# Exponentiating the first batch's keys before the transpose instead of after the maximum

## The chip, the cores and the metric

The kernel runs on one core of one Trainium2 chip. The metric is the device time of one execution in microseconds (us). The kernel before took a median of 944.75 us over three runs (944.59, 944.75 and 946.4).

Five engines of the core matter here. TensorE (PE in the profile, PEld for its weight loads) multiplies and transposes, VectorE (DVE) and ScalarE (ACT) do the elementwise work, GpSimd (POOL) fills constants and issues some DMAs, and SyncE (SP) issues most of the DMAs.

## The reference

A linear attention feeds a gated layer. All arrays are float32.

```python
batch, n_heads, seq, head_dim = (8, 8, 576, 64)
n_tokens, d_model, d_ff = (4608, 512, 1536)

q_s = np.exp(q - np.max(q, axis=-1, keepdims=True))
q_s = q_s / (np.sum(q_s, axis=-1, keepdims=True) + 1e-09)
k_s = np.exp(k - np.max(k, axis=2, keepdims=True))
k_s = k_s / (np.sum(k_s, axis=2, keepdims=True) + 1e-09)
kv = np.einsum('bhsd,bhse->bhde', k_s, v)
x = np.einsum('bhsd,bhde->bhse', q_s, kv)
# heads are joined to 512 features per token; x is (4608, 512)
gate = 1.0 / (1.0 + np.exp(-(x @ w_gate)))
out = (gate * (x @ w_val)) @ w_out
```

The queries are normalised over the 64 features of a head, the keys over the 576 positions of a batch. `max` and `sum` of the keys therefore run along the sequence.

## The kernel before, in words

The 4608 tokens are cut into nine windows of 512 (`w`, `T`). Each window needs its attention output `x` (512 features by 512 tokens, four tiles of 128 features), and then the layer: twelve blocks `j` of 128 hidden units, each with a gate and a value product (`g1_0`, `g1`) and a product back (`g2_0`, `g2`) into four PSUM accumulators.

Windows 1 to 8 run a scheme with fewer block products and split operands; they make up the span from about 162 us on. Window 0 runs plainly (`g1_0(j)`, `g2_0(j)`, lines 644 to 682) because at its time the weights are still being loaded and narrowed. The weights arrive as 64-bit words; `w_low`, `w_top` and `w_join` (and `wo_low`, `wo_top`, `wo_join`) turn them into float32, partly on VectorE, partly on ScalarE. While TensorE works on window 0, those two engines narrow, sum and split the weights of all twelve blocks.

Order is written out by hand: each engine executes its instructions in the order of the code, and SP issues its DMAs in the order of the code. At most eight of SP's DMAs are in flight: the ninth waits until the first has landed, and so on. The loads at the start are, in order: batch 0's keys `k0` (positions on partitions, two tiles per DMA), its queries `q0`, the first weights `w_raw(0)`, batch 0's values `v0`, then `wo(0)`, `w(1)`, `wo(1)`, `w(2)`, batch 1's transposed keys, `w(3)`, `wo(2)`, window 1's queries; after the start stage `w(4)`, batch 1's keys, and from block to block one `wo` and one `w`.

The start stage is what lies ahead of `g1_0(0)`, lines 909 to 1029. With positions on partitions the keys' maximum has to run across partitions. So VectorE takes the maximum over the five position tiles (L960, L963), TensorE transposes the result (L966), VectorE reduces it (L971) and spreads it on a diagonal (L974), TensorE multiplies the diagonal by ones to have the maxima on all partitions (L980), and VectorE subtracts them from each tile (L379) before ScalarE exponentiates it (L384). The queries are treated between these steps: `qn_max` (L473), `qn_sub` (L480), `qn_exp` (L484), `qn_sum` (L490 to L496), `qf_mul` (L521), and `qf_tr` (L527) transposes them. `k_mm_0` (L392) multiplies keys by values, two groups `g` of two feature tiles; the values carry one column of ones more per head pair (129 columns), whose result is the keys' sum. `k_done_0` (L423 to L415) divides by that sum. `x_mm_0` (L589) multiplies by the queries, and `x_ev_0` takes the result out of PSUM as `x_0`, on which `g1_0(0)` works.

`warm(n)` (L955) issues n products of ones that nobody reads. A float32 product stands in the profile as two matmuls, a transpose as one.

Of the kernel before, what the change touches and what calls it, by code (L numbers as in the profile page):

```python
# [52 lines left out]
def attn_moe(ctx: ExitStack, tc: tile.TileContext, qf, qn, qT, k, kT, v, wg, wv, wo, out):  # L53
# [297 lines left out]
    def k_load(b, t, kt=None):  # L351
        s0, n = KTILES[t]
        if kt is None:
            kt = ring.tile([P, DM], F32, name="ring")
        nc.sync.dma_start(out=kt[:n], in_=k[b, s0:s0 + n])
        kt_sb[b, t] = kt

    def v_load(b, t, vt=None):
# [8 lines left out]
        src = v[b, s0:s0 + n]
        if b == 0:
            nc.sync.dma_start(out=vt[:n, :, 0:P], in_=src.rearrange("s (h e) -> s h e", e=P))
        else:  # L370
            nc.sync.dma_start(out=vt[:n], in_=src)

    def k_sub(b, t, eng=nc.vector):
        n = KTILES[t][1]
        kt, m = kt_sb[b, t][:n], kmb[b][:n]
        if b > 0:
            kt = kt.rearrange("s (h p) -> s h p", p=P)
            m = m.rearrange("s (p h) -> s h p", h=NP)
        eng.tensor_tensor(out=kt, in0=kt, in1=m, op=ALU.subtract)  # L379

    def k_exp(b, t):
# [2 lines left out]
        nc.scalar.activation(kt[:n], kt[:n], AF.Exp)  # L384

    def k_mm_0(t, g, ps):

        n = KTILES[t][1]
        kt, vt = kt_sb[0, t], v_sb[0, t]
        for i in range(2):  # L390
            hp = 2 * g + i
            nc.tensor.matmul(  # L392
                ps[:, i], lhsT=kt[:n, hp * P:(hp + 1) * P], rhs=vt[:n, hp],
                start=(t == 0 and i == 0), stop=(t == len(KTILES) - 1 and i == 1),
                skip_group_check=True,
            )
# [73 lines left out]
    def qn_max(w, c):  # L470
        if c == 0:
            q_m[w] = const.tile([P, NC * TI, 1], F32, name="q_m")
        nc.vector.tensor_reduce(  # L473
            out=q_m[w][:, c * TI:(c + 1) * TI], in_=qn_sb[w, c], axis=AX.X, op=ALU.max
        )

    def qn_sub(w, c, eng=nc.vector):
        t = qn_sb[w, c]
        m = q_m[w][:, c * TI:(c + 1) * TI]
        eng.tensor_tensor(out=t, in0=t, in1=m.broadcast_to([P, TI, D]), op=ALU.subtract)  # L480

    def qn_exp(w, c):
        t = qn_sb[w, c]
        nc.scalar.activation(t, t, AF.Exp)  # L484
# [436 lines left out]
    for t in (ones, v0[:, :, :, P:VW]):  # L921
        nc.gpsimd.memset(t, 1.0)

    for t in range(0, 4, 2):
        rows = k[0, t * P:(t + 2) * P].rearrange("(t p) e -> p t e", p=P)
        nc.sync.dma_start(out=k0[:, t:t + 2], in_=rows)
        kt_sb[0, t], kt_sb[0, t + 1] = k0[:, t], k0[:, t + 1]
    k_load(0, 4, k0[:, 4])
    for c in range(0, NC, 2):
        nc.sync.dma_start(out=q0[:, c:c + 2], in_=qf[0, c:c + 2].rearrange("c p t -> p c t"))  # L930
    for c in range(NC):
        qn_sb[0, c] = q0[:, c].rearrange("p (i d) -> p i d", d=D)
# [20 lines left out]
    def warm(n):  # L953
        for _ in range(n):
            nc.tensor.matmul(idle[:, 0:P], lhsT=ones, rhs=ones, start=True, stop=True)  # L955
# [4 lines left out]
    nc.vector.tensor_tensor(out=top, in0=k0[:, 0], in1=k0[:, 1], op=ALU.max)  # L960
    for t in range(2, 5):
        n = KTILES[t][1]
        nc.vector.tensor_tensor(out=top[:n], in0=top[:n], in1=kt_sb[0, t][:n], op=ALU.max)  # L963
    ps = ps_acc.tile([P, DM], F32, name="acc")
    for hp in range(NP):
        nc.tensor.transpose(ps[:, hp * P:(hp + 1) * P], top[:, hp * P:(hp + 1) * P], ident)  # L966
    warm(6)
    qn_max(0, 0)
    qn_max(0, 1)
    m = const.tile([P, NP, 1], F32, name="kmax_0")  # L970
    nc.vector.tensor_reduce(  # L971
        out=m, in_=ps.rearrange("p (h s) -> p h s", s=P), axis=AX.X, op=ALU.max
    )
    nc.vector.tensor_tensor(  # L974
        out=diag.rearrange("p (h s) -> p h s", s=P),
        in0=ident.unsqueeze(1).broadcast_to([P, NP, P]),
        in1=m.broadcast_to([P, NP, P]), op=ALU.mult,
    )
    kmb[0] = ps_acc.tile([P, DM], F32, name="acc")
    nc.tensor.matmul(kmb[0], lhsT=ones, rhs=diag, start=True, stop=True)  # L980
    qn_max(0, 2)
    qn_max(0, 3)
    for c in range(NC):
        qn_sub(0, c)
    for c in range(2):
# [1 line left out]
    k_sub(0, 0, nc.vector)
    nc.scalar.copy(out=wide, in_=kmb[0])
    k_exp(0, 0)
    kmb[0] = wide  # L990
# [200 lines left out]
```

## Time and profile before

| what | value |
|---|---|
| median of three runs | 944.75 us |
| the profiled execution's own time | 946.96 us |
| its span, first to last instruction | 945.2 us |
| around the span (946.96 less 945.2) | 1.76 us |
| mean granted TensorE clock | 0.994 |
| PE busy over the span | 933.5 us, 99% |
| first matmul of `g1_0(0)` starts at | 31.77 us |

The profile is one execution. A row of a group gives line, engine, operation, output and inputs by the program's names, shapes, the count (x), then the time busy in us, the mean in ns of one, and the engine's idle time ahead of them with what ended it. A row of the timeline or of the chain of waits gives the start in us from the start of the span, the length in us, and what ran. A row of a table by stage gives the stretch, busy time per engine with counts in brackets, the granted TensorE clock (1.00 is full), the DMA engines' busy share, and GB/s moved. L12 is line 12 of the kernel. A DMA row gives the KB of one and the us from issue to landing.

### The profile page before, as it was taken

The page shows a single profiled execution, that of the slowest core. Times are in us where ns is not written, and L with a number is a line of the kernel's source. Part 1 is how long each engine was busy: PE and PEld are TensorE (multiplying, and loading weights), DVE is VectorE, ACT ScalarE, POOL GpSimd, SP SyncE. Part 2 cuts the span into 40 slices and gives each one's busy share as a digit, 9 for nine tenths or more (in the row PEclk, how much of TensorE's full clock was granted, in tenths as well). Part 3 has the DMA queues.
Part 4 walks back from the last instruction along what each step waited for, and adds up shares of the span by engine and source line. Part 5 has one row for each costly group of instructions (what it writes and reads, how often), then busy time and mean ns, then how long its engine had stood idle before and what let it go on. Part 6 is the DMA issues. An engine that isn't in the chain of part 4 may idle for free.

```text
span 945.2 us, 15707 instructions
## 1 busy us (share of the span) xinstructions
PE 933.5 (99%) x6062; PEld 808.2 (86%) x6062; DVE 626.4 (66%) x1017; ACT 485.4 (51%) x822; POOL 176.5 (19%) x330
## 2 busy tenths in 40 slices
PE   6999999999999999999999999999999999999998
PEld 5545545899999999999999999999999999999997
DVE  8899879874767477755776568556856664654242
ACT  4799786635455445544563456254725443543222
POOL 0011112222121212212221122112212122222220
PEclk8999999999999999999999999999999999999999
DMA  9996576999699969996999699978997789858661
GB/s 323 328 392 226 210 288 237 362 342 272 185 372 320 264 183 354 335 266 208 333 331 283 204 309 344 287 246 252 351 266 229 221 258 314 238 177 262 212 212 67
DMA packets 94249, 256.74 MB, mean 272 GB/s; under 512 B 13600, under 2 KB 15904, under 8 KB 94176
## 3 DMA queue, kind: packets, MB, share of 16 engines
q0 software_dynamic: 46016, 167.27, 56.6%
q1 hardware_dynamic: 48160, 88.48, 30.9%
q8 instruction: 48, 0.79, 0.4%
q14 instruction: 25, 0.20, 0.1%
HBM read 227.15 MB, written 28.56 MB: 271 GB/s over the span
## 4 chain that ended last, share of the span: by engine, by line
PE 98%; DVE 1%; DMA 1%; ACT 0%; issue 0%; SPq 0%; DVEq 0%
PE gv L695 49%; PE acc L763 28%; PE gv L650 9%; PE acc L677 4%; PE at L405 3%; PE gv L565 2%; PE at L565 1%; PE acc L392 1%; DMA lent<-k_in 1%; PE acc L589 0%; PE gv L527 0%; DVE lent L480 0%; DVE q_m L473 0%; DVE lent L963 0%; ACT lent L384 0%; ACT lent L484 0%
## 5 line engine op out<-in xcount | busy, mean ns | idle before, releaser
L695 PE MATMUL gv<-c_hl,s_sb 128*128 128x256 f32 x2304 | 277.6, 276 | 0.0
L695 PEld LDWEIGHTS gv<-c_hl,s_sb 128*128 128x128 f32 x2304 | 269.1, 188 | 0.0
L695 PE MATMUL gv<-c_hl,a_w 128*128 128x256 f32 x1728 | 221.0, 277 | 0.0
L695 PEld LDWEIGHTS gv<-c_hl,a_w 128*128 128x128 f32 x1728 | 210.5, 188 | 4.6 <-issue 0.7
L301 POOL DMA_DIRECT2D s_sb<-s x188 | 101.3, 539 | 306.2 <-PE gv L695 299.8
L721 DVE TENSOR_TENSOR sg<-gv,sg 128x512 f32<-128x512 f32 x48 | 33.2, 691 | 167.5 <-PE gv L695 167.5
L763 PE MATMUL acc<-wo_hl,h 128*128 128x512 f32 x588 | 142.4, 391 | 0.0
L763 PE MATMUL acc<-wo_t,h 128*128 128x512 f32 x564 | 138.9, 394 | 0.0
L763 PEld LDWEIGHTS acc<-wo_t,h 128*128 128x128 f32 x564 | 105.8, 188 | 24.8
L763 PEld LDWEIGHTS acc<-wo_hl,h 128*128 128x128 f32 x588 | 106.9, 188 | 20.7
L713 ACT COPY sg<-gv 128x512 f32<-128x512 f32 x48 | 28.1, 585 | 118.1 <-PE gv L695 104.7
L723 ACT COPY sg<-gv 128x512 f32<-128x512 f32 x48 | 28.2, 587 | 102.8 <-PE gv L695 102.8
L725 DVE TENSOR_TENSOR sg<-sg 128x512 f32<-128x512 f32 x48 | 33.2, 692 | 57.1 <-ACT sg L723 57.1
L650 PE MATMUL gv<-x,f_w 128*128 128x512 f32 x160 | 70.3, 593 | 0.0
L248 POOL DMA_DIRECT2D wo_hl<-wo x47 | 27.6, 588 | 194.8 <-PE acc L763 194.8
L650 PEld LDWEIGHTS gv<-x,f_w 128*128 128x128 f32 x160 | 30.0, 190 | 36.6 <-issue 34.4
L746 DVE TENSOR_TENSOR h<-sg,h 128x1024 fp32r<-128x1024 f32 x48 | 58.8, 1226 | 1.6
L734 DVE TENSOR_TENSOR sg<-sg 128x512 f32<-128x512 f32 x48 | 33.2, 692 | 33.5 <-ACT sg L728 33.5
L728 ACT ACTIVATE sg<-sg 128x512 f32<-128x512 f32 x48 | 30.3, 632 | 46.1 <-DVE sg L727 46.1
L718 ACT COPY sg<-gv 128x512 f32<-128x512 f32 x48 | 28.2, 587 | 37.3 <-PE gv L695 37.3
L715 ACT COPY sg<-gv 128x512 f32<-128x512 f32 x48 | 28.2, 587 | 36.5 <-PE gv L695 36.5
L248 POOL DMA_DIRECT2D wo_t<-wo x47 | 25.3, 538 | 99.2 <-PE acc L763 99.1
(153 smaller groups left out, 1151.3 us busy)
## 6 DMA issues: line engine op xcount, KB each, us to landing
s_sb<-s POOLq DMA_DIRECT2D x188, 512.0 KB, 6.2
wo_hl<-wo POOLq DMA_DIRECT2D x47, 512.0 KB, 5.0
wo_t<-wo POOLq DMA_DIRECT2D x47, 512.0 KB, 6.6
s<-s_sb POOLq DMA_DIRECT2D x24, 512.0 KB, 6.7
out<-x SPq DMA_DIRECT2D x36, 256.0 KB, 7.0
ring<-k_in SPq DMA_DIRECT2D x28, 256.0 KB, 9.5
ring<-qn_in SPq DMA_DIRECT2D x28, 256.0 KB, 6.0
q_b<-q_m_row SPq DMA_DIRECT2D x56, 128.0 KB, 9.4
```

What stands on the lines that cost most here:

```text
L248: nc.gpsimd.dma_start(out=t.rearrange("p h e -> p (h e)"), in_=wo_dram[2 * p + i].bitcast(F32R))
L301: nc.gpsimd.dma_start(out=s_sb[:, i].rearrange("p h n e -> p (h n e)"), in_=s_dram[p][:, i * n:(i + 1) * n].bitcast(F32R),)
L405: nc.tensor.matmul(kvps[b][:, hp], lhsT=kt[:n, sl], rhs=vt[:n, sl], start=(t == 0 and hp == 0), stop=(t == len(KTILES) - 1 and hp == NP - ...
L650: nc.tensor.matmul(ps[n], lhsT=w[:, kt // 2, sl], rhs=x_0[:, kt], start=(kt == 0), stop=(kt == NK - 1),)
L677: nc.tensor.matmul(acc[0][m], lhsT=h_0[j][:, m * P:(m + 1) * P], rhs=wo_t[j // 2][:, j % 2], start=(j == 0), stop=(j == NJ - 1),)
L695: nc.tensor.matmul(ps[:, n], lhsT=lh(kt), rhs=c_hl[i][:, x, kt], start=(first and n == 0 and kt == 0 and lh is wh and x == 0), stop=(last ...
L721: nc.vector.tensor_tensor(out=sg[:, 0], in0=rr, in1=sg[:, 0], op=ALU.add)
L725: nc.vector.tensor_tensor(out=sg[:, 3], in0=sg[:, 3], in1=sg[:, 2], op=ALU.add)
L728: nc.scalar.activation(sg[:, 0:2, 0], sg[:, 0:2, 0], AF.Sigmoid)
L734: tt(out=sg[:, 0:2, 0], in0=sg[:, 0:2, 0], in1=sg[:, 0:2, 1], op=ALU.mult)
L746: nc.vector.tensor_tensor(out=lo, in0=sg[:, :, 0], in1=hi.bitcast(F32), op=ALU.subtract)
L763: nc.tensor.matmul(acc[w][m], lhsT=h[lh][:, i, sl], rhs=o[i][:, rh], start=(at == 0 and i == 0 and lh == 0 and rh == 0), stop=(at == NS - ...
```

## The change

Batch 0's keys are now read with features on partitions, `kT`, one DMA for each of the four feature tiles of 128 features by 576 positions, and the loads alternate: two key tiles, two query tiles, two key tiles, two query tiles. The maximum now runs along the free axis: `k_max` (a reduction and a negation on VectorE) and `k_sum` (one exponential on ScalarE, with the maximum as bias and the sum as a second result). The exponentiated tile is then transposed by TensorE, four full pieces of 128 positions and one of 64 (`k_tr_0`), and ScalarE copies it from PSUM (`k_get_0`). The sum comes with the exponential, so the values lose their column of ones: 128 columns instead of 129, and their DMA writes rows of 2048 bytes per partition instead of four of 512.

The filling matmuls are dealt out anew: 11 at the start and 8 after each pair, instead of 16 and 6. `k_mm_0` runs through the position tiles inside a feature tile, no longer through feature tiles inside a position tile. VectorE clears a quarter of `f_last` instead of the whole.

```diff
-    nc.vector.memset(f_last, 0.0)
+    nc.vector.memset(kv_0, 0.0)
     nc.vector.tensor_copy(
-        out=kv_sb.rearrange("p b i h e -> p (b i h e)"),
-        in_=f_last.rearrange("p b n e -> p (b n e)"),
+        out=kv_sb.rearrange("p b i h e -> p (b i) (h e)"),
+        in_=kv_0.rearrange("p h e -> p (h e)").unsqueeze(1).broadcast_to([P, 4, DM]),
     )
...
-        if b == 0:
-            nc.sync.dma_start(out=vt[:n, :, 0:P], in_=src.rearrange("s (h e) -> s h e", e=P))
-        else:
-            nc.sync.dma_start(out=vt[:n], in_=src)
+        nc.sync.dma_start(out=vt[:n], in_=src)
...
+    def k_tr_0(hp):
+        if hp % 2 == 0:
+            k_ps["end", hp // 2] = ps_gv.tile([P, T], F32, name="gv")
+        k_ps[hp] = ps = ps_acc.tile([P, DM], F32, name="acc")
+        for t, (s0, n) in enumerate(KTILES):
+            if n == P:
+                o = ps[:, t * P:(t + 1) * P]
+            else:
+                o = k_ps["end", hp // 2][:n, hp % 2 * P:(hp % 2 + 1) * P]
+            nc.tensor.transpose(o, kT_sb_0[hp][:, s0:s0 + n], ident)
+
+    def k_get_0(hp):
+        nc.scalar.copy(out=k0[:, hp], in_=k_ps.pop(hp))
+        if hp % 2:
+            n = KTILES[-1][1]
+            nc.scalar.copy(
+                out=k0_end[:n, hp - 1:hp + 1].rearrange("s h d -> s (h d)"),
+                in_=k_ps.pop(("end", hp // 2))[:n, 0:2 * P],
+            )
+
+    def k_mm_0(g, ps):
         for i in range(2):
             hp = 2 * g + i
-            nc.tensor.matmul(
-                ps[:, i], lhsT=kt[:n, hp * P:(hp + 1) * P], rhs=vt[:n, hp],
-                start=(t == 0 and i == 0), stop=(t == len(KTILES) - 1 and i == 1),
+            for t, (s0, n) in enumerate(KTILES):
+                kt = k0[:, hp, t * P:(t + 1) * P] if n == P else k0_end[:n, hp]
+                nc.tensor.matmul(
+                    ps[:, i], lhsT=kt, rhs=v_sb[0, t][:n, hp * P:(hp + 1) * P],
+                    start=(t == 0 and i == 0), stop=(t == len(KTILES) - 1 and i == 1),
...
-        k_r = const.tile([P, NP], F32, name="k_r0")
-        nc.vector.tensor_scalar_add(k_r[:, gs].unsqueeze(2), ps[:, :, P:VW], EPS)
-        nc.vector.reciprocal(k_r[:, gs], k_r[:, gs])
+        k_r = ksum[0]
+        if g == 0:
+            nc.vector.tensor_scalar_add(k_r, k_r, EPS)
+            nc.vector.reciprocal(k_r, k_r)
...
+    kT_sb_0 = [k0T[:, hp] for hp in range(NP)]
+    for i in range(0, NP, 2):
+        for hp in (i, i + 1):
+            nc.sync.dma_start(out=k0T[:, hp], in_=kT[0, hp * P:(hp + 1) * P])
+            kT_load(0, hp, k0T[:, hp])
+        for c in (i, i + 1):
+            nc.sync.dma_start(out=q0[:, c], in_=qf[0, c])
+            qn_sb[0, c] = q0[:, c].rearrange("p (i d) -> p i d", d=D)
...
-    warm(16)
+    warm(11)
+
+    for i in range(0, NP, 2):
+        for hp in (i, i + 1):
+            k_max(0, hp)
+            k_sum(0, hp)
+            k_tr_0(hp)
+        for c in (i, i + 1):
+            qn_max(0, c)
+            qn_sub(0, c)
+            qn_exp(0, c)
+            k_get_0(c)
+        warm(8)
     w_low(0)
-    for c in range(2, NC):
-        qn_exp(0, c)
-    for t in range(1, 5):
-        k_exp(0, t)
     w_top(0)
-    kv0 = [ps_acc.tile([P, 2, VW], F32, name="acc") for _ in range(2)]
+    kv0 = [pool.tile([P, 2, P], F32, name=name) for pool, name in ((ps_at, "at"), (ps_acc, "acc"))]
     for g in range(2):
-        for t in range(5):
-            k_mm_0(t, g, kv0[g])
+        k_mm_0(g, kv0[g])
...
-        qf_tr(0, hp, ps_gv.tile([P, T], F32, name="gv") if hp < 3 else
-              ps_at.tile([P, T], F32, name="at"))
+        qf_tr(0, hp, ps_gv.tile([P, T], F32, name="gv"))
```

Left out of the diff are the removed lines of the old maximum (lines 960 to 997 of the kernel before, printed above) and of the old loads of keys and queries, and the places in the lent tiles.

What the order of instructions becomes on TensorE, from the last filling matmuls ahead of the keys-by-values product to `x_mm_0`. Before (L955 is `warm`, L980 the spreading of the maxima, L392 `k_mm_0`, L527 `qf_tr`, L589 `x_mm_0`):

```order
L955 MATMUL gv<-lent 128x128 x6
L980 MATMUL acc<-lent 128x512
L392 MATMUL acc<-lent 128x129 x20
L527 MATMUL gv<-ident,lent 128x128 x12
L527 MATMUL at<-ident,lent 128x128 x4
L589 MATMUL acc<-q_151,f_last 128x512 x2
```

Now (L393 is the transpose of the keys, L971 `warm`, L409 `k_mm_0`, L545 `qf_tr`, L607 `x_mm_0`):

```order
L393 MATMUL acc<-ident,lent 128x128 x4
L393 MATMUL gv<-ident,lent 64x128
L971 MATMUL gv<-lent 128x128 x8
L409 MATMUL at<-lent 128x128 x10
L409 MATMUL acc<-lent 128x128 x10
L545 MATMUL gv<-ident,lent 128x128 x16
L607 MATMUL acc<-q_151,f_last 128x512 x2
```

The single product that spread the maxima, and the wait for it, are gone from TensorE; eight filling matmuls now stand directly ahead of the keys-by-values product, whose columns are 128.

On VectorE, from the subtraction of the queries' maxima to the first scaling of the queries. Before (L480 `qn_sub`, L379 `k_sub`, L146 `w_low(0)`, L490 to L496 `qn_sum`, L521 `qf_mul`):

```order
L480 TENSOR_TENSOR lent<-lent,q_m 128x512 x4
L379 TENSOR_TENSOR lent<-lent,acc 128x512
L379 TENSOR_TENSOR lent<-lent 128x512 x3
L379 TENSOR_TENSOR lent<-lent 64x512
L146 TENSOR_SCALAR w_raw<-w_raw 128x1024
L490 TENSOR_REDUCE q_r<-lent 128x8 x4
L495 TENSOR_SCALAR q_r<-q_r 128x32
L496 RECIPROCAL q_r<-q_r 128x32
L521 TENSOR_TENSOR lent<-lent,q_r 128x512 x2
```

Now (L498 `qn_sub` of the last query tile, L145 `w_low(0)`, L508 to L514 `qn_sum`, L539 `qf_mul`):

```order
L498 TENSOR_TENSOR lent<-lent,q_m 128x512
L145 TENSOR_SCALAR w_raw<-w_raw 128x1024
L508 TENSOR_REDUCE q_r<-lent 128x8 x4
L513 TENSOR_SCALAR q_r<-q_r 128x32
L514 RECIPROCAL q_r<-q_r 128x32
L539 TENSOR_TENSOR lent<-lent,q_r 128x512 x2
```

The five subtractions of the keys' maxima are gone; the narrowing of the first weights follows directly on the queries.

More of the change, by code (lines that the diff above doesn't have):

```diff
@@ L33 @@
 KTILES = [(i * P, min(P, S - i * P)) for i in range((S + P - 1) // P)]
-VW = P + 1
 NF = 2
@@ L375, in k_sub @@
         kt, m = kt_sb[b, t][:n], kmb[b][:n]
-        if b > 0:
-            kt = kt.rearrange("s (h p) -> s h p", p=P)
-            m = m.rearrange("s (p h) -> s h p", h=NP)
+        kt = kt.rearrange("s (h p) -> s h p", p=P)
+        m = m.rearrange("s (p h) -> s h p", h=NP)
         eng.tensor_tensor(out=kt, in0=kt, in1=m, op=ALU.subtract)
@@ L384, in k_exp @@
         nc.scalar.activation(kt[:n], kt[:n], AF.Exp)
-    def k_mm_0(t, g, ps):
-        n = KTILES[t][1]
-        kt, vt = kt_sb[0, t], v_sb[0, t]
+    k_ps = {}
+    def k_tr_0(hp):
[17 more added lines that the diff above has]
+    def k_mm_0(g, ps):
         for i in range(2):
             hp = 2 * g + i
-            nc.tensor.matmul(
-                ps[:, i], lhsT=kt[:n, hp * P:(hp + 1) * P], rhs=vt[:n, hp],
-                start=(t == 0 and i == 0), stop=(t == len(KTILES) - 1 and i == 1),
-                skip_group_check=True,
-            )
+            for t, (s0, n) in enumerate(KTILES):
[3 more added lines that the diff above has]
+                    start=(t == 0 and i == 0), stop=(t == len(KTILES) - 1 and i == 1),
+                    skip_group_check=True,
+                )
     def k_mm(b, t):
@@ L910, in attn_moe @@
     k1T = lent[5][:, 0:NP * S].rearrange("p (h s) -> p h s", s=S)
-    k0 = lent[4][:, 0:5 * DM].rearrange("p (t e) -> p t e", e=DM)
-    ones = lent[4][:, 5 * DM:5 * DM + P]
+    k0T = lent[4][:, 0:NP * S].rearrange("p (h s) -> p h s", s=S)
+    ones = lent[4][:, NP * S:NP * S + P]
+    k0 = lent[0][:, 0:NP * 4 * P].rearrange("p (h s) -> p h s", s=4 * P)
+    k0_end = lent[0][:, NP * 4 * P:NP * 5 * P].rearrange("p (h d) -> p h d", d=P)
     q0 = lent[3][:, 0:NC * T].rearrange("p (c t) -> p c t", t=T)
-    top, diag = (lent[3][:, NC * T + i * DM:NC * T + (i + 1) * DM] for i in range(2))
-    v0 = lent[2][:, 0:5 * NP * VW].rearrange("p (t h e) -> p t h e", t=5, e=VW)
-    wide = lent[0][:, 0:DM]
+    v0 = lent[2][:, 0:5 * DM].rearrange("p (t e) -> p t e", e=DM)
     v1 = [
@@ L920, in attn_moe @@
     ]
[L921 to L932, printed above, removed]
+    nc.gpsimd.memset(ones, 1.0)
+    kT_sb_0 = [k0T[:, hp] for hp in range(NP)]
[6 more added lines that the diff above has]
+            qn_sb[0, c] = q0[:, c].rearrange("p (i d) -> p i d", d=D)
     load_w(0)
@@ L955, in warm @@
             nc.tensor.matmul(idle[:, 0:P], lhsT=ones, rhs=ones, start=True, stop=True)
-    warm(16)
[L960 to L985, printed above, removed]
-        qn_exp(0, c)
[L987 to L990, printed above, removed]
-    for t in range(1, 5):
-        k_sub(0, t)
+    warm(11)
[10 more added lines that the diff above has]
+        warm(8)
     w_low(0)
-    for c in range(2, NC):
-        qn_exp(0, c)
-    for t in range(1, 5):
-        k_exp(0, t)
     w_top(0)
-    kv0 = [ps_acc.tile([P, 2, VW], F32, name="acc") for _ in range(2)]
+    kv0 = [pool.tile([P, 2, P], F32, name=name) for pool, name in ((ps_at, "at"), (ps_acc, "acc"))]
     for g in range(2):
-        for t in range(5):
-            k_mm_0(t, g, kv0[g])
+        k_mm_0(g, kv0[g])
     for c in range(NC):
```

## The prediction

> **What bounds the kernel now.** I read the page first, then the chain of waits over the first 100 us, then a table by stage of the same time.
>
> ```profile
> PE 933.5 (99%) x6062; PEld 808.2 (86%) x6062; DVE 626.4 (66%) x1017; ACT 485.4 (51%) x822; POOL 176.5 (19%) x330
> PE   6999999999999999999999999999999999999998
> ```
>
> TensorE is busy everywhere but in the first of 40 slices. So a change of the start stage is worth what it moves the moment from which TensorE never waits again. The chain says when that is:
>
> ```profile
> 12.38 2.40 DVE lent L480 x4
> ...
> 18.14 8.46 PE acc L392 x36
> 26.60 1.46 PE gv L527 x12
> 28.06 0.44 PE at L527 x4
> 28.50 3.44 PE acc L589 x8
> 31.93 13.73 PE gv L650 x32
> ```
>
> Up to 18 us VectorE's maxima and subtractions end last, with ScalarE's exponentials; then `k_mm_0` holds TensorE. Everything from 31.93 on is TensorE alone. Two things beside it show in the stages (the third last column is the granted clock, the last is GB/s):
>
> ```profile
> 4.00:8.00 4.00, 2.96 (x21) 2.77 (x19) 2.42 (x5) 0.00 (x0) 0.00 (x0) 1.00 1.06 348
> 12.00:16.00 4.00, 0.37 (x1) 0.00 (x0) 3.38 (x6) 1.82 (x4) 0.00 (x0) 0.95 1.24 285
> 20.00:24.00 4.00, 4.00 (x18) 3.55 (x17) 3.83 (x10) 3.03 (x3) 0.00 (x0) 0.50 1.02 406
> 24.00:28.00 4.00, 4.00 (x27) 3.67 (x26) 2.51 (x8) 0.78 (x2) 0.00 (x0) 0.77 1.05 397
> 33.00:36.00 3.00, 3.00 (x8) 1.33 (x7) 2.96 (x7) 3.00 (x4) 0.00 (x0) 1.00 0.64 171
> 32.00:100.00 68.00, 68.00 (x191) 32.74 (x190) 66.60 (x117) 64.14 (x84) 8.15 (x15) 1.00 0.85 309
> ```
>
> First, TensorE sat idle ahead of `k_mm_0` and ran it at a granted clock of 0.50. Second, VectorE is busy 66.60 of the 68 us from 32 to 100: it narrows weights with hardly a gap. Whatever makes VectorE wait there is not made up before 100 us.
>
> **The change, part by part.** The prices of the new work are those of like operations in this trace:
>
> ```profile
> L330 DVE TENSOR_REDUCE k_max<-lent 128x1 f32<-128x576 f32 x4 | 3.0, 740 | 0.0
> L331 DVE TENSOR_SCALAR k_neg<-k_max 128x1 f32<-128x1 f32 x6 | 0.9, 154 | 0.2
> L473 DVE TENSOR_REDUCE q_m<-lent 128x8 f32<-128x512 f32 x4 | 2.5, 672 | 0.0
> L480 DVE TENSOR_TENSOR lent<-lent,q_m 128x512 f32<-128x512 f32 x4 | 2.5, 682 | 0.0
> L146 DVE TENSOR_SCALAR w_raw<-w_raw 128x1024 uint32<-128x1024 uint32 x2 | 1.4, 682 | 0.0
> L490 DVE TENSOR_REDUCE q_r<-lent 128x8 f32<-128x512 f32 x4 | 2.4, 668 | 0.0
> L521 DVE TENSOR_TENSOR lent<-lent,q_r 128x512 f32<-128x512 f32 x4 | 2.6, 689 | 0.1
> L415 DVE TENSOR_TENSOR f_last<-acc,k_r 64x128 f32<-64x128 f32 x4 | 1.2, 289 | 0.1
> L337 ACT ACTIVATE lent<-lent,k_neg 128x576 f32<-128x576 f32 x4 | 3.0, 761 | 0.0
> L484 ACT ACTIVATE lent<-lent 128x512 f32<-128x512 f32 x4 | 2.4, 624 | 3.5 <-DVE lent L480 3.5
> L484 ACT ACT_TABLE_LOAD x1 | 1.3, 1283 | 8.2 <-DMA lent<-qf_in 8.2
> L596 ACT COPY x<-acc 128x512 f32<-128x512 f32 x2 | 1.2, 586 | 1.7 <-PE acc L589 1.7
> ```
>
> *The first keys.* The first load of 512 KB, issued at 0.74, took 3.8 us. A key tile is 288 KB, 0.23 MB less; at the 0.4 MB per us of the stage rows it lands 0.6 earlier, at about 4.0.
>
> ```profile
> 0.74 0.43 SPq L926 DMA_DIRECT2D lent<-k_in  x1
> lent<-k_in SPq DMA_DIRECT2D x1, 512.0 KB, 3.8
> 9.47 2.52 SPq L369 DMA_DIRECT2D lent<-v_in  x1
> lent<-v_in SPq DMA_DIRECT2D x1, 128.0 KB, 7.2
> 90.30 4.66 PE at L405 x40
> ```
>
> *VectorE.* From 4.0 it works without a gap, as the other tiles land 0.7 apart: maxima 3.0, negations 4 x 0.15 = 0.6, queries 2.5 + 2.5, narrowing half of 1.4 = 0.7, sums 2.4, scaling 2.6, four small steps at about 0.2 (like the negations' 0.15) 0.8, the results 1.2. Together 16.3, so it ends at 20.3 and has scaled the last query tile at 19.7, half of the results earlier.
>
> *ScalarE.* From 4.0: the table 1.3, exponentials 3.0 + 2.4, copies at most 6 x 0.59: 10.2, so 14.2, with waits for VectorE about 14.8. It hides behind the values, below; were they there, it would be the next to end.
>
> *The values.* The last landed at 9.47 + 7.2 = 16.7. While they moved, the rows show 285 GB/s, after it 406; 1.18 MB take 4.1 us at the one and 2.9 at the other. In rows of 2048 bytes, as the rest is, they land 1.2 earlier, at 15.5. In the Trainium skill, "DMA: Bandwidth & Descriptors", section Specifications, 512 bytes already suffice for line rate; the 285 against 406 speaks against it here, and by the page the values would still land at 16.7 (a rival, below).
>
> *TensorE.* `k_mm_0` is 40 matmuls; at the full clock L405 gives 4.66/40 = 0.117 each, against 8.46/36 = 0.235 in the chain above. Four of the first five products can run ahead; 32 matmuls after 15.5 end at 19.2. The sixteen transposes take 1.46/12 = 0.12 each, 1.9 in all: `x_mm_0` starts at 21.1 (VectorE's last query tile would allow 20.2). Against 28.50 this is **7.4 us earlier**. The 20 transposes of keys, 2.4 us, fall before 13 us, where TensorE otherwise fills. Bounds: values landing another 0.6 earlier because the 348 of 4 to 8 us also rises to 406, then 20.5 decides, 8.0; values no earlier, 22.3, 6.2.
>
> *What costs nothing.* The fill and cast of `kv_sb` end before the first keys land, as they did (the cast with a repeated source could take twice its time and still would). `x_ev_0`, `w_join` and the rest move along with `x_mm_0`.
>
> *What does not move along: the loads.* SP's queue holds the same bytes in the same order behind the values. The narrowing meets `wo(3)` first:
>
> ```profile
> 37.61 0.33 SPq L138 DMA_DIRECT2D wo_raw<-wo_in  x1
> wo_raw<-wo_in SPq DMA_DIRECT2D x1, 512.0 KB, 6.5
> 44.85 0.42 DVE L146 TENSOR_SCALAR wo_raw<-wo_raw 128x512 uint32<-128x512 uint32 x1
> 84.58 0.68 DVE L662 TENSOR_TENSOR h<-gv,h 128x512 f32<-128x512 f32 x1
> 86.70 0.59 PE L677 MATMUL acc<-wo_t,h 128*128 128x512 f32 x1
> ```
>
> It landed at 44.1, 0.75 before VectorE read it. What it gains: 1.2 from the values, and the thin stretch from 33 to 36 (171 of 400 GB/s, 1.7 us), since `w(4)` waits for VectorE and is issued earlier. That gives 41.2. The other end: 14.2 MB lie up to it (keys and queries 2.2, values 1.2, five w 5.2, four wo 2.1, batch 1's keys twice 2.4, window 1's queries 1.1), at 0.4 MB per us from 2.5 us on 37.9. Nothing tells where between; I take the middle, **39.6**. VectorE then reads it 44.85 - 39.6 = 5.25 earlier, not 7.4, and stays that late. TensorE feels it where VectorE's lead is least: the product at 84.58 ends at 85.26 and its reader starts at 86.70, a lead of 1.44. So TensorE keeps 5.25 + 1.44 = **6.7 us** of the 7.4.
>
> *The sum.* 946.96 - 6.7 = **940.3**. The profiled execution is 2.2 above the median of 944.75 and 0.6 above the longest of the three. The half-clock stretch would account for it: without it `k_mm_0` would not be last, VectorE's last scaling and four transposes would, and `x_mm_0` would start at 25.64 + 0.5, 2.4 earlier.
>
> ```profile
> 24.35 1.29 DVE L521 TENSOR_TENSOR lent<-lent,q_r 128x512 f32<-128x512 f32 x2
> ```
>
> The new kernel is reckoned without that stretch, so its time stands; from the median it is 4.5 away.
>
> **Rivals.**
>
> *No backlog.* The queue runs near its best, or VectorE's lead absorbs the rest: the whole 8.0 arrives, 939.0; if the profiled execution's surplus over the median is the profiler's, 944.75 - 8.0 = 936.8. For it: 0.75 of lead today, and 406 GB/s where rows are long. Against: the lead is smaller than the 7.4 that VectorE moves.
>
> *The values' rows were not it.* 285 GB/s had another cause, and the values land at 16.7: `wo(3)` at 42.4, VectorE gains 2.45, TensorE 3.9: 943.1. The DMA share of 1.24 in that row, the highest, speaks for short rows.
>
> *Slower: the half clock stays.* At the start the clock is not full either:
>
> ```profile
> 1.14 5.82 PE L955 MATMUL gv<-lent 128*128 128x128 f32 x32 [1.14 <-POOL lent L922]
> 16.63 0.77 PE L392 MATMUL acc<-lent 128*128 128x129 f32 x2 [4.26 <-ACT lent L384]
> ```
>
> 32 matmuls took 0.18 each, between the 0.117 and the 0.235: they became fast on the way. Now there are 22, and behind them come short bursts. If these do not bring the full clock, `k_mm_0` takes 40 x 0.235 = 9.4 from 15.8 on, and the rest 1.9 + 3.44: 30.5, a gain of 1.4, 945.5. If the half clock also holds through `qf_tr` and `x_mm_0` (3.8 + 6.9), `g1_0(0)` starts at 35.9, 4.0 later than before: **951.0**. It decides whether the granted clock is 0.50 still at 27 us. Against it: the gaps between bursts are under 2 us, where a gap of 4.26 took the clock away. For it: before, the clock came back only after 7.6 us of steady matmuls (18.14 to about 25.8, by the 0.77). The Trainium skill, "TensorE: Matmul & The Clock Gate", Part 1, gives about 3.4 us of busy time for that, which this trace more than doubles; by the page the first 22 matmuls, 5.2 us at 0.235, bring the full clock and the forecast stands. Part 4 says that transposes do not count as busy, which no run here shows and which would leave these bursts thinner.
>
> **How the numbers follow.** Forecast, full clock with a backlog: 0.60, 939.6 (all 7.4) to 941.9 (`wo(3)` at 41.2). No backlog 0.17. Short rows innocent 0.05. Half clock through `k_mm_0` 0.09, further 0.05. Something unseen 0.04, mostly still a gain. The range takes in the forecast and the low rival's 936.8 and reaches up to the short rows' 943.1: 936.8 to 943.1. About 0.2% (1.9 us) is what a measurement of this kernel can tell from no change. Faster 0.60 + 0.17 + 0.03 = 0.80; within it 0.05 + 0.09 = 0.14; slower 0.06.
>
> **What would show it.** `k_mm_0` at 0.117 per matmul with the granted clock at 1.00 from 12 us on; `x_mm_0` at 21.1; VectorE's idle time ahead of `wo(3)`'s narrowing ended by a DMA, and a short TensorE wait at the fifth product back. I am wrong if `x_mm_0` starts after 23, if VectorE does not wait for a load between 29 and 40 us, or if the clock reads 0.50 after 15 us.

## The result, and the profile after

The changed kernel is slower: 956.2 us as the median of its first measurement against 944.79 for the kernel before, a ratio of 1.0115 with a 95% interval of 1.0095 to 1.0135. One of the four executions, the profiled one, took 4422.31 us with every matmul several times as long; it is left out, and the profile read here is that of the same kernel run again (e1_again: 955.72, ratio 1.0093 [1.0072, 1.0114]). Its span is 953.7 us, 8.5 more than before.

The stages of the start first (stretch; busy time of PE, PEld, DVE, ACT and POOL; granted clock; DMA share; GB/s):

```profile
4.00:8.00 4.00, 3.81 (x27) 3.45 (x26) 3.50 (x7) 3.81 (x7) 0.00 (x0) 1.00 1.03 335
12.00:16.00 4.00, 3.25 (x28) 2.87 (x25) 3.97 (x7) 3.79 (x6) 0.00 (x0) 1.00 1.06 359
20.00:24.00 4.00, 4.00 (x30) 3.40 (x29) 1.55 (x4) 1.56 (x3) 0.00 (x0) 1.00 1.03 399
24.00:28.00 4.00, 4.00 (x11) 1.74 (x10) 3.24 (x6) 2.40 (x3) 0.00 (x0) 1.00 1.04 406
33.00:36.00 3.00, 3.00 (x9) 1.33 (x8) 2.90 (x8) 2.99 (x4) 0.00 (x0) 1.00 1.03 404
32.00:100.00 68.00, 67.43 (x190) 32.28 (x189) 65.74 (x115) 62.08 (x83) 8.68 (x16) 1.00 0.84 308
```

The start stage moved as forecast in kind: the clock reads 1.00 in every one of these stages, the thin stretch from 33 to 36 us now moves 404 GB/s instead of 171, and from 12 to 16 us TensorE is busy for 3.25 us instead of 0.37. (The thin stretch is not the change's alone: a run of the kernel before with the same start instructions, e7 below, whose clock came back earlier, moves 405 there. An earlier start is enough to fill it.) The timeline of TensorE gives the moments (start, length):

```profile
23.41 3.60 PE L607 MATMUL acc<-q,f_last 128*128 128x512 f32 x8
26.84 1.02 PE L668 MATMUL gv<-x,f_w 128*128 128x512 f32 x2
...
157.98 1.95 PE L713 MATMUL gv<-c_hl,a_w 128*128 128x256 f32 x12
159.78 3.00 PE L713 MATMUL gv<-c_hl,s_sb 128*128 128x256 f32 x24
```

The same matmuls of the kernel before:

```profile
28.33 3.60 PE L589 MATMUL acc<-q,f_last 128*128 128x512 f32 x8
31.77 0.59 PE L650 MATMUL gv<-x,f_w 128*128 128x512 f32 x1
162.08 1.15 PE L695 MATMUL gv<-c_hl,a_w 128*128 128x256 f32 x5
```

`x_mm_0` starts 4.9 us earlier, and when windows 1 to 8 begin, at the first product with `c_hl`, 4.1 us of it are still there. Yet the end is 8.5 us later. So 12.6 us were lost behind 158 us, in code that the diff doesn't touch. The groups by line say where. Before:

```profile
L695 PE MATMUL gv<-c_hl,s_sb 128*128 128x256 f32 x2304 | 277.6, 276 | 0.0
L695 PE MATMUL gv<-c_hl,a_w 128*128 128x256 f32 x1728 | 221.0, 277 | 0.0
L763 PE MATMUL acc<-wo_hl,h 128*128 128x512 f32 x588 | 142.4, 391 | 0.0
L763 PE MATMUL acc<-wo_t,h 128*128 128x512 f32 x564 | 138.9, 394 | 0.0
```

And after:

```profile
L713 PE MATMUL gv<-c_hl,s_sb 128*128 128x256 f32 x2304 | 288.1, 281 | 0.0
L713 PE MATMUL gv<-c_hl,a_w 128*128 128x256 f32 x1728 | 222.5, 278 | 0.0
L781 PE MATMUL acc<-wo_hl,h 128*128 128x512 f32 x588 | 142.5, 391 | 0.0
L781 PE MATMUL acc<-wo_t,h 128*128 128x512 f32 x564 | 138.9, 394 | 0.0
```

Same shapes, same counts, no idle time ahead of them, no lower clock (a mean of 1.000 after, 0.994 before): 10.5 us more in the products of `s_sb` (the weights) with `c_hl` (the moving data), 1.5 more in those of `a_w` with `c_hl`, nothing in the products back. Together 12.0 of the 12.6. In the chain of waits the 84 matmuls of a step stand as one piece, before

```profile
211.26 9.52 PE gv L695 x84
...
226.31 9.52 PE gv L695 x84
```

and after

```profile
207.41 9.80 PE gv L713 x84
...
222.73 9.80 PE gv L713 x84
```

which is 113.3 against 116.7 ns per matmul, averaged over a step (9.52/84 and 9.80/84). A step has 48 products of `s_sb` and 36 of `a_w`. By the starts of the matmuls in the trace, one to the next, the former went from 113.7 to 118.3 ns and the latter from 113.9 to 114.7, on average over the whole run. What the change does to these matmuls stands in two lines of the diff that carry no work: the tiles `kmax_0` (L970) and `k_r0` (L422) of the kernel before, 32 bytes per partition each, are gone. Pools are laid out one behind the other, so everything allocated behind these two lies 64 bytes lower in each partition, `c_hl` and `a_w` among it; `s_sb`, the first tile, stays. (All places here are added up from the tiles of the kernel's code; the profile shows none. `c_hl` is several tiles; by its start the first of them is meant, and the others lie multiples of 128 bytes behind it.)

### The profile page after: what moved, and what is told of

Its sections match the earlier page's. It is cut to its first block, busy times and chain, and to the rows that moved or that the text cites. A ratio compares the mean times of both kernels' runs of the same rounds, so it can differ in the third digit from the quotient of the medians.

```text
span 4420.5 us, 15759 instructions
## 1 busy us (share of the span) xinstructions
PE 4415.4 (100%) x6086; PEld 3418.9 (77%) x6086; DVE 626.5 (14%) x1012; ACT 494.3 (11%) x830; POOL 174.1 (4%) x329
## 4 chain that ended last, share of the span: by engine, by line
PE 100%; ACT 0%; issue 0%; POOL 0%; POOLq 0%
PE gv L713 47%; PE acc L781 27%; PE gv L668 11%; PE acc L695 6%; PE at L422 4%; PE gv L583 2%; PE at L583 1%; PE gv L971 1%; PE acc L607 0%; PE gv L545 0%; PE acc L409 0%; PE at L409 0%; PE acc L393 0%; PE gv L393 0%; ACT x L687 0%
## 5 line engine op out<-in xcount | busy, mean ns | idle before, releaser
L713 PE MATMUL gv<-c_hl,s_sb 128*128 128x256 f32 x2304 | 1222.4, 830 | 0.0
L713 PEld LDWEIGHTS gv<-c_hl,s_sb 128*128 128x128 f32 x2304 | 1213.7, 742 | 0.0
L713 PEld LDWEIGHTS gv<-c_hl,a_w 128*128 128x128 f32 x1728 | 931.4, 731 | 39.5 <-issue 37.4
L713 PE MATMUL gv<-c_hl,a_w 128*128 128x256 f32 x1728 | 946.1, 840 | 0.0
L781 PE MATMUL acc<-wo_hl,h 128*128 128x512 f32 x588 | 617.8, 1337 | 0.0
L781 PE MATMUL acc<-wo_t,h 128*128 128x512 f32 x564 | 586.8, 1327 | 0.0
L781 PEld LDWEIGHTS acc<-wo_t,h 128*128 128x128 f32 x564 | 348.3, 618 | 224.0 <-issue 224.0
L781 PEld LDWEIGHTS acc<-wo_hl,h 128*128 128x128 f32 x588 | 362.8, 634 | 196.2 <-issue 191.9
L668 PE MATMUL gv<-x,f_w 128*128 128x512 f32 x160 | 426.3, 3011 | 0.0
L668 PEld LDWEIGHTS gv<-x,f_w 128*128 128x128 f32 x160 | 143.8, 905 | 264.8 <-issue 263.0
L739 DVE TENSOR_TENSOR sg<-gv,sg 128x512 f32<-128x512 f32 x48 | 33.2, 691 | 1901.9 <-PE gv L713 1901.9
L695 PE MATMUL acc<-wo_t,h 128*128 128x512 f32 x96 | 258.4, 3043 | 0.0
L695 PEld LDWEIGHTS acc<-wo_t,h 128*128 128x128 f32 x96 | 89.1, 933 | 161.1 <-issue 161.1
L422 PE MATMUL at<-f_last,ring 128*128 128x128 f32 (+1 forms) x160 | 92.4, 875 | 0.0
L422 PEld LDWEIGHTS at<-f_last,ring 128*128 128x128 f32 (+1 forms) x160 | 88.3, 780 | 4.3 <-issue 4.3
L743 DVE TENSOR_TENSOR sg<-sg 128x512 f32<-128x512 f32 x48 | 33.2, 692 | 291.2 <-ACT sg L741 291.2
```

The costliest lines, as they stand in the source:

```text
L422: nc.tensor.matmul(kvps[b][:, hp], lhsT=kt[:n, sl], rhs=vt[:n, sl], start=(t == 0 and hp == 0), stop=(t == len(KTILES) - 1 and hp == NP - ...
L668: nc.tensor.matmul(ps[n], lhsT=w[:, kt // 2, sl], rhs=x_0[:, kt], start=(kt == 0), stop=(kt == NK - 1),)
L695: nc.tensor.matmul(acc[0][m], lhsT=h_0[j][:, m * P:(m + 1) * P], rhs=wo_t[j // 2][:, j % 2], start=(j == 0), stop=(j == NJ - 1),)
L713: nc.tensor.matmul(ps[:, n], lhsT=lh(kt), rhs=c_hl[i][:, x, kt], start=(first and n == 0 and kt == 0 and lh is wh and x == 0), stop=(last ...
L739: nc.vector.tensor_tensor(out=sg[:, 0], in0=rr, in1=sg[:, 0], op=ALU.add)
L743: nc.vector.tensor_tensor(out=sg[:, 3], in0=sg[:, 3], in1=sg[:, 2], op=ALU.add)
```

## The experiments

**First, is it one execution, and do the fills matter?** The changed kernel unchanged; with more filling matmuls; without the second fills; and the kernel before with the shorter first fill.

> The changed kernel once more, for a profile that stands beside its timed runs of 955.7 to 956.6 us. Theory clock (TensorE's short bursts of filling matmuls, 11, 8 and 8 pairs, do not bring the full clock, so that window 0 begins at half clock): matmuls of the keys-by-values product 0.21 us apart, 512-column matmuls 0.86 apart for some 30 us, time 955 to 957. Theory backlog (my forecast's mechanism, much larger than I sized it): 128-column matmuls 0.11 apart from 6 us on, x_mm_0 at 21 to 22 us, and TensorE idle for over 15 us in all inside window 0, behind VectorE that waits for loads.

> The changed kernel with more filling matmuls: 18 at the start instead of 11, and 20 after each pair of tiles instead of 8, so that TensorE has no idle stretch ahead of the keys-by-values product. Theory clock: the clock is released early and stays, 938 to 943 us. Theory backlog: the fill changes nothing that ends last, 955 to 958 us.

```diff
-    warm(11)
+    warm(18)
...
-        warm(8)
+        warm(20)
```

> The changed kernel without the two bursts of 8 filling matmuls; the 11 at the start stay. Theory clock: the half clock lasts at least as long as in the changed kernel, 955 to 960 us. Theory backlog: as the changed kernel within 1 us.

```diff
-        warm(8)
```

> The kernel before with 11 filling matmuls at the start instead of 16, nothing else. Theory clock: if 11 are too few to release the clock, its start stage is lengthened too, by 2 to 12 us over 944.8. Theory backlog: 944.8 within 1 us.

```diff
-    warm(16)
+    warm(11)
```

Measured: 955.72; 957.45 (1.0113 [1.0088, 1.0137]); 959.23 (1.013 [1.0105, 1.0155]); 946.11 (1.0 [0.9985, 1.0014]). The group of `s_sb` with `c_hl` stayed at 288.1 us in the first three and at 277.6 in the fourth: the loss is in each of the three profiles, and no filling touches it. So neither theory of these expectations, clock or backlog, accounts for it. The fills only move the start. With more of them TensorE itself is late and `x_mm_0` starts at 26.53; without the second ones the granted clock is 0.50 from 12 to 20 us, and it starts at 25.82. Both other doses were slower than the one in the change.

**Is it the 64 bytes?** The changed kernel with 64 unused bytes behind `ident`, where everything behind returns to its old place; with the same 64 bytes ahead of `s_sb`, where `c_hl` returns to its old place but `s_sb` moves along; the kernel before with its two small tiles put into a buffer that exists anyway, so that its `c_hl` moves down; and the changed kernel with 32 bytes. The first of these is called the padded kernel from here on.

> The changed kernel with one unused tile of 64 bytes per partition in the pool of the constants, so that everything behind it (c_hl, a_w, the operands of the products back) lies where it lay before; s_sb lies ahead of it and does not move. Theory places (the change took two small tiles out of that pool, moved everything behind by 64 bytes, and the matmuls that pair s_sb with c_hl run 4.7 ns slower for it, 2304 of them, those with a_w 1.1 ns slower, 1728 of them: 12.7 us): s_sb matmuls back at 113.5 ns apart, time 955.7 - 12.7 = 943.0. Theory start stage (the new start and its order cost the time): 955.7 within 1 us.

```diff
     ident = const.tile([P, P], F32, name="ident")
+    const.tile([P, 16], F32, name="pad_c")
```

> The changed kernel with the same unused 64 bytes, but ahead of s_sb: c_hl, a_w and the rest lie where they lay before, and s_sb is moved along, so that the distance from s_sb to c_hl is that of the changed kernel. If the distance between the two operands decides: 118 ns, 955 to 956 us. If the place of c_hl, a_w and the rest by itself decides: 113.5 ns, 943. Theory start stage: 955.7.

```diff
+    const.tile([P, 16], F32, name="pad_c")
     s_sb = const.tile([P, 4, 2, 2, 2 * P], F32R, name="s_sb")
```

> The kernel before, whose two small tiles (the keys' maximum and the inverse of the keys' sum) now lie in a lent tile: same instructions, everything behind the constants 64 bytes lower, as in the changed kernel. Theory places: 944.9 + 12.7 = 957.6. Theory start stage: 944.9 within 1 us.

```diff
-        k_r = const.tile([P, NP], F32, name="k_r0")
+        k_r = lent[0][:, DM + 16:DM + 16 + NP]
...
-    m = const.tile([P, NP, 1], F32, name="kmax_0")
+    m = lent[0][:, DM:DM + NP].rearrange("p (h one) -> p h one", one=1)
```

> The changed kernel with 32 unused bytes behind s_sb instead of 64. Theory places: between the two, or at one of them, which tells how fine the step is: 943 to 956, with the spacing of the s_sb matmuls between 113.5 and 118.2 ns to match. Theory start stage: 955.7.

```diff
+    const.tile([P, 8], F32, name="pad_c")
```

Measured: 944.91 (0.9997 [0.9986, 1.0008]); 956.64 (1.0123 [1.0108, 1.0139]); 957.11 (1.0133 [1.0118, 1.0149]); 958.94 (1.0155 [1.0136, 1.0174]). The two that decide, the changed kernel with the pad behind `ident`:

```profile
L714 PE MATMUL gv<-c_hl,s_sb 128*128 128x256 f32 x2304 | 277.5, 276 | 0.0
L714 PE MATMUL gv<-c_hl,a_w 128*128 128x256 f32 x1728 | 220.9, 277 | 0.0
```

and the kernel before with its tiles moved:

```profile
L695 PE MATMUL gv<-c_hl,s_sb 128*128 128x256 f32 x2304 | 288.1, 281 | 0.0
L695 PE MATMUL gv<-c_hl,a_w 128*128 128x256 f32 x1728 | 222.5, 278 | 0.0
```

The loss goes with the 64 bytes in both directions, to 0.1 us in each group, whatever the start stage looks like. That the pad ahead of `s_sb` doesn't help shows that the place of `c_hl` alone doesn't decide. What counts is its place relative to `s_sb`, or to a tile that moves along with `s_sb`; that it is `s_sb`, the slowed products' own weights, is the likeliest reading and not shown apart. The distance from `c_hl` to `a_w` never changed, so the 1.5 us of that group come from elsewhere; from what, no run shows. Two times missed their expectations: with 64 bytes the kernel took 944.91 and not 943.0 (the reason comes under the start, below), and with 32 bytes it was slower than with none, not between the two.

**Which distance is good?** Two more: 128 bytes behind `ident` (with 32 less in a later pad, to fit), and the pad of 64 with the small tile `q_m` put ahead of `s_sb`, which moves `s_sb` up by 128 and leaves the rest.

> The changed kernel with 128 bytes more in the constants, so that c_hl begins 60928 bytes behind s_sb (60864 in the kernel before, 60800 in the changed kernel, 60832 with 32 bytes). Theory A (what counts is the distance modulo 128): s_sb against c_hl at 118 ns per matmul as in the changed kernel, 955 to 957. Theory B (modulo 256 or the exact bank): 113.5 ns, 944 to 946. A third: something between, as other pairs move as well.

```diff
+    const.tile([P, 32], F32, name="pad_c")
...
-    fpad.tile([P, 16], F32, name="pad_f")
+    fpad.tile([P, 8], F32, name="pad_f")
```

> The padded kernel with the small tile q_m put ahead of s_sb: c_hl and everything behind it stay where they are, s_sb moves up by 128 bytes, so that c_hl begins 60736 bytes behind it. So far the distance 60864 ran at 113.7 ns per matmul, and 60800, 60832 and 60928 at 118.3 to 119.9. Theory A (distances that leave 64 modulo 128 are good): 113.7 ns, 944 to 946. Theory B (the good distance is one modulo 256 or more): 118 ns or more, 954 to 966.

```diff
+    const.tile([P, NC * TI, 1], F32, name="q_m")
     s_sb = const.tile([P, 4, 2, 2, 2 * P], F32R, name="s_sb")
...
+    const.tile([P, 16], F32, name="pad_c")
```

They took 964.8 (1.0205 [1.0192, 1.0219]) and 943.45 (0.9984 [0.9973, 0.9995]). The groups with 128 bytes:

```profile
L714 PE MATMUL gv<-c_hl,s_sb 128*128 128x256 f32 x2304 | 291.9, 283 | 0.0
L714 PE MATMUL gv<-c_hl,a_w 128*128 128x256 f32 x1728 | 225.9, 280 | 0.0
```

and with `q_m` ahead:

```profile
L715 PE MATMUL gv<-c_hl,s_sb 128*128 128x256 f32 x2304 | 277.5, 276 | 0.0
```

| start of `c_hl` less start of `s_sb`, bytes | left over modulo 128 | `s_sb` with `c_hl`, us | runs |
|---|---|---|---|
| 60736 | 64 | 277.5 | e13 |
| 60800 | 0 | 288.1 | e1, e6, e7 |
| 60832 | 32 | 291.9 | e8 |
| 60864 | 64 | 277.5 to 277.6 | before, e5 |
| 60928 | 0 | 291.9 | e11 |

Both distances that leave 64 are quick, the three others are not. The table fits a rule modulo 128, for this pair, but five distances don't prove one, and the next run limits it. It doesn't explain why 60928 is worse than 60800: with 128 bytes the time lay above both theories, the `a_w` group, too, took 4.9 us more than before, and `wo_hl` 1.6 more (144.0), though neither had its distance to its moving data changed.

**Does the rule hold for another pair?** The padded kernel with the output weights 64 bytes nearer to `h`.

> The padded kernel with the output weights' tiles (wo_t, wo_hl) 64 bytes nearer to h, and everything else where it is (16 words less in one pad, 16 more in another). The products back take 229 ns (wo_hl) and 232 ns (wo_t) per matmul of 512 columns, 1152 of them. Theory A (any pair of weights and moving data is quickest at 64 modulo 128; here the distance is 0 now and becomes 64): up to 2 to 5 ns less per matmul, 939 to 943. Theory B (these pairs were placed well already, or it holds for s_sb and c_hl alone): the same or slower, 944.9 to 952.

```diff
-    wpad.tile([P, 32], F32, name="pad_w")
+    wpad.tile([P, 16], F32, name="pad_w")
...
-    fpad.tile([P, 16], F32, name="pad_f")
+    fpad.tile([P, 32], F32, name="pad_f")
```

959.72 us (1.0147 [1.0131, 1.0164]), outside both theories: the hope of theory A fell, and something else came up.

```profile
L714 PE MATMUL gv<-c_hl,s_sb 128*128 128x256 f32 x2304 | 285.7, 280 | 0.0
L714 PE MATMUL gv<-c_hl,a_w 128*128 128x256 f32 x1728 | 227.1, 281 | 0.0
L782 PE MATMUL acc<-wo_hl,h 128*128 128x512 f32 x588 | 145.7, 397 | 0.0
L782 PE MATMUL acc<-wo_t,h 128*128 128x512 f32 x564 | 136.8, 392 | 0.0
```

Of the moved pairs one became slower by 3.2 us and one quicker by 2.1. The products of `c_hl`, none of whose operands moved, lost 8.2 and 6.2. So the table's distance doesn't decide alone: this run has 60864, as the kernel before, and 285.7 us. The run's chain of waits shows how:

```profile
188.47 9.53 PE gv L714 x84
...
208.39 9.89 PE gv L714 x84
...
223.84 9.89 PE gv L714 x84
```

and that of the padded kernel at the same steps:

```profile
188.80 9.89 PE gv L714 x84
...
209.09 9.52 PE gv L714 x84
...
224.13 9.52 PE gv L714 x84
```

The same 84 matmuls run at either 9.52 or 9.89 us, 113.3 or 117.7 ns each, through a whole step, and the next products back, whose operands e14 moved, lie between them. That the step's rate is set by what ran just ahead of it fits, and was not tried alone. It is not the loss of e1 over again: in a slow step of e14 the products of `s_sb` and those of `a_w` are 117.8 ns apart alike, in a step of e1 118.3 and 114.5.

**Where is the gain of the start?** With the 64 bytes put back the kernel equals the one before (0.9997), though `x_mm_0` starts at 23.06. By the first product with `c_hl` (160.11) only 2.0 of the 5.3 us are left. TensorE and VectorE of the padded kernel:

```profile
83.82 1.12 PE L696 MATMUL acc<-wo_t,h 128*128 128x512 f32 x2 [1.44 <-DVE h L681]
```

```profile
43.32 0.43 DVE L146 TENSOR_SCALAR wo_raw<-wo_raw 128x512 uint32<-128x512 uint32 x1 [3.69 <-DMA wo_raw<-wo_in]
```

VectorE sits 3.69 us ahead of `wo(3)`, and TensorE waits for VectorE's product at the fifth product back: the backlog of the forecast. To test it, the second batch's queries and keys, 2.2 MB that nobody reads before 47 us in either kernel, were asked for behind `wo(3)` and `w(5)`, in the padded kernel and, for comparison, in the kernel before.

> The padded kernel (944.91, the changed kernel with 64 bytes put back) with the second batch's loads of queries (qn_load(1)) and keys (k_load(1)) asked for after block 0's loads of wo(3) and w(5), not ahead of them. In the padded kernel wo(3) lands at 43.30, VectorE idles 3.69 us for it, TensorE idles 1.44 us at the second products' fourth block and 2.1 in all before the first c_hl, and its lead over the kernel before shrinks from 5.3 to 2.0 us. Theory A (the backlog of loads gives the early start back): 2.1 MB less stand ahead of wo(3), it lands before 39, VectorE's wait falls below 0.5 us, TensorE keeps 2 us or more of the lead: 941.5 to 943.3. Theory B (the lead is lost to VectorE's and ScalarE's own work, the load was only the last to come): the wait for wo(3) goes, the lead at the first c_hl stays at 2: 944 to 945.5.

> The kernel before, with the second batch's loads of queries and keys behind wo(3) and w(5) as in the run with the loads later. Theory A (that move pays only because the changed start outruns the loads): in the kernel before VectorE doesn't wait for wo(3), 944.5 to 945.5, and the difference to the run with the loads later (942.43) is the start's gain without the backlog. Theory B (the move helps any kernel): 942 to 943.5, and the change brings nothing even with the backlog out of the way.

```diff
-    for c in range(NC):
-        qn_load(1, c)
...
-    for t in range(5):
-        k_load(1, t)
...
     def after_first(j):
         if j == 0:
+            for c in range(NC):
+                qn_load(1, c)
+            for t in range(5):
+                k_load(1, t)
```

942.43 (0.9977 [0.996, 0.9994]) and 945.15 (0.9998 [0.9987, 1.0008]): theory A in both. In the first TensorE doesn't wait at all, as its stage row says, beside that of the padded kernel without the move:

```profile
32.00:100.00 68.00, 68.00 (x192) 32.75 (x191) 66.41 (x116) 61.52 (x83) 8.69 (x16) 1.00 0.86 320
```

```profile
32.00:100.00 68.00, 65.87 (x184) 30.92 (x183) 63.36 (x112) 60.48 (x81) 8.18 (x15) 1.00 0.82 304
```

The pair gives what the changed start is worth when neither the bytes nor the backlog are in the way: 945.15 - 942.43 = 2.7 us, between medians.

**What sets the start?** The values ahead of `w(0)`; that with the loads later; and that with the narrowing of `w(0)` behind `qn_sum`.

> The padded kernel with the five loads of values ahead of the load of w(0). The values now land at 16.26 and k_mm_0 runs from 13.9 to 21.3. 1 MB less ahead of them is about 2.5 us: if the values' landing sets the start stage (theory A), the last value lands at about 13.8, k_mm_0 ends at 19, x_mm_0 starts at 20.6 to 21.5 instead of 23.06; the loads behind are as late as before, so that wo(3) still lands at 43.3 and TensorE's idle before the first c_hl grows by as much: 944 to 945.5. Theory B (the arrival of data isn't what bounds the stage): x_mm_0 stays at 22.5 to 23.5, 944.9. If the time falls by more than 1 us, the backlog doesn't take the start back.

```diff
-    load_w(0)
     for t in range(5):
         v_load(0, t, v0[:, t])
+    load_w(0)
```

> Both edits: values ahead of w(0), and the second batch's queries and keys behind wo(3) and w(5), with the 64 bytes put back. If the values' landing sets the start and the backlog gives it back (theory A of both), the two gains add: x_mm_0 at about 21, no wait for wo(3) over 1 us, 939.5 to 941.8, which would be faster than the kernel before by 0.3 to 0.5%. If the lead is lost to the engines' own work (theory B), 944 to 945.5.

> The version with values first and the second batch's loads later (942.79), with the narrowing of w(0) (w_low(0), w_top(0)) put behind the four sums of the first batch's queries (qn_sum) in the order of VectorE and ScalarE. Theory A (in the run with values first k_mm_0 ended 2.0 us earlier, and the start didn't follow because VectorE's queue stood behind w(0)'s landing at 15.8): x_mm_0 starts at 20.8 to 22 instead of 23.5, 940 to 942. Theory B (the chain of VectorE's own work to x sets the start whatever lands first): x_mm_0 at 23 to 24, 942 to 943.5.

```diff
-    w_low(0)
-    w_top(0)
...
     for c in range(NC):
         qn_sum(0, c)
+    w_low(0)
+    w_top(0)
```

943.91 (0.9984 [0.9976, 0.9993]), 942.79 (0.9977 [0.9967, 0.9988]) and 940.59 (0.9948 [0.9936, 0.9961]). The first missed its own forecast: `k_mm_0` ended 1.9 us earlier, at 19.39, but `x_mm_0` started at 23.80, later than without the edit, because VectorE's queue stood behind `w(0)`:

```profile
15.93 0.70 DVE L146 TENSOR_SCALAR w_raw<-w_raw 128x1024 uint32<-128x1024 uint32 x1 [3.56 <-DMA w_raw<-wv_in]
16.54 0.68 DVE L509 TENSOR_REDUCE q_r<-lent 128x8 f32<-128x512 f32 x1
```

The second missed, too: its `x_mm_0` starts at 23.50, behind the same wait (2.78 us), and the two gains don't add (942.79 against 942.43 with the loads later alone). With the sums ahead of that wait (e15):

```profile
12.50 2.46 DVE L509 TENSOR_REDUCE q_r<-lent 128x8 f32<-128x512 f32 x4
...
16.29 0.70 DVE L146 TENSOR_SCALAR w_raw<-w_raw 128x1024 uint32<-128x1024 uint32 x1 [0.73 <-DMA w_raw<-wv_in]
```

`x_mm_0` starts at 21.56. This version, 940.59 us, beats both kernels. So the values' landing set the start of the changed kernel, and once they came earlier VectorE's order did.

## Why the prediction was wrong

**The failing step is "What costs nothing".** It named the work that is filled in or moves along, and passed over the two small tiles that the diff removes. That step was worth +12.0 us (10.5 in `s_sb`, 1.5 in `a_w`), more than the 7.4 us that the start was to gain. It is shown: put back, the loss goes; taken from the kernel before, it comes. Why 64 bytes matter to these products is open. None of the rivals had it either; "something unseen" held 0.04. It was not the only fault: with the bytes put back the time is 944.91, still above the forecast's upper end of 943.1, through the terms that follow.

**The start, 7.4 us.** The kind was right and the size was not: 28.33 to 23.41 and 23.06 (e5) is 4.9 to 5.3. Two terms were mis-sized. The values landed at 16.26 to 16.61, not at 15.5: longer rows brought 359 GB/s (318 in e5) instead of 285 into the stage from 12 to 16 us, but the last of them landed 0.1 to 0.4 us earlier instead of 1.2. The load ahead of them landed at 12.11 before, 12.52 in e1 and 12.18 in e5, and from there they took 4.1 us instead of 4.6. The rows were the right suspect, against the rival that held them innocent: a packet of 512 bytes took 33.2 ns in the kernel before and one of 2048 bytes 97.5 in e5, which is 15.4 against 21.0 bytes per ns and DMA engine. That the loads behind, which move at the same time, take up the rest of the gain fits, and was not tried. And the products behind them were priced at 0.117 each, where in e5 they take

```profile
16.31 1.99 PE L410 MATMUL at<-lent 64*128 64x128 f32 x12 [0.17 <-DMA lent<-v_in]
18.23 3.08 PE L410 MATMUL acc<-lent 128*128 128x128 f32 x20
```

5.0 us for 32, 0.156 each at a granted clock of 1.00, 1.3 more than the 3.7 of the sum; why L405's price didn't carry over, no run shows. 0.76 and 1.3 on the 21.1 make 23.2.

**The base.** The profiled execution of the kernel before was 2.2 us above the median, and the text put that to the half-clock stretch. That held. The moved kernel before (e7), with the same instructions, had a clock of 0.93 from 20 to 24 us where the profiled one had 0.50, and

```profile
29.64 0.59 PE L650 MATMUL gv<-x,f_w 128*128 128x512 f32 x1
```

stands 2.13 us ahead of the 31.77. Against such an execution the changed start gains 3.1 us (26.50), not 5.3. The forecast said so itself (4.5 us from the median, where its sum takes 6.7 off the profiled execution); only the 2.4 us that it gave the stretch came out as 2.1.

**The clock.** Right: 1.00 in every stage of e1 and e5 from 4 us on. The rival with the half clock came up only when the second fills were taken out (e3).

**The backlog.** Right in its mechanism and in the load that comes late (`wo(3)`; in e5 also in the fifth product back, which waits for it); the landing of `wo(3)` was mis-sized: `wo(3)` landed at 41.23 in e1 and at 43.30 in e5, not at 39.6, VectorE waited for 1.27 and 3.69 us, and in e5 TensorE lost 2.1 in waits of its own (1.44, 0.58 and 0.12). So the middle between the bounds was the wrong choice: e1 is at the upper end, 41.2, and e5 beyond it. Of the lead at `x_mm_0`, 0.7 of 7.4 us was to be lost; up to the first product with `c_hl` e1 lost 0.8 of 4.9 and e5 3.3 of 5.3. The two kernels have the same loads in the same order, so part of this may be how far executions differ. The rival without a backlog is refuted by the same rows.

**By its own test** the prediction was wrong at `x_mm_0` (23.41 in e1, after 23), VectorE's wait for the load came at 40, on the edge of what was named, and nothing in that test could have shown the larger loss, since it looked at no row behind 100 us.

## What to carry to other kernels

Before saying that an edit leaves a saturated loop alone, look at the addresses: a removed or added tile of 32 bytes shifts every pool behind it, and in a kernel that is 99% matmuls, 4% on one pair of operands (118.3 against 113.7 ns) is more than the whole gain of the start stage. Compare the groups by line with their counts between the two traces first: the same count with a longer time and no idle is no matter of waits. And an earlier start is worth only what the queues behind it can follow: ask which load is next, and whether a queue stands behind one that isn't needed yet.
